# Routed attention and a feed-forward layer on one core: four late placements moved, and one batch's feed-forward pieces dealt unevenly

## The chip, the cores and the metric

The kernel runs on one NeuronCore of a Trainium2 chip. The core has a matrix engine (TensorE, PE in the profile), a vector engine (VectorE, DVE), a scalar engine (ScalarE, ACT), GpSimd (POOL) and a sync engine (SyncE, SP), which here only issues transfers. Each works through its own queue of instructions in the order in which they were written down, and engines wait for each other by semaphores. The metric is the device time of one execution in microseconds (us), and lower is better. The kernel before takes 940.79 us (median of 3 runs, 940.7 to 941.31).

## The reference

Two stages follow each other. The first is attention with routing: 4 batches, 8 heads, 768 tokens, 64 numbers per token and head. Every query and every key is assigned to the one of 16 centroids with which its direction agrees best, and a query attends only to keys of its own cluster.

```python
q_assign = np.argmax(np.einsum('bhsd,hcd->bhsc', q_n, c_n), axis=-1)
k_assign = np.argmax(np.einsum('bhsd,hcd->bhsc', k_n, c_n), axis=-1)
mask = q_assign[:, :, :, None] == k_assign[:, :, None, :]
scores = np.where(mask, scale * np.matmul(q, k.transpose(0, 1, 3, 2)), -1e9)
attn = softmax(scores)
x = np.matmul(attn, v)             # heads side by side: 3072 tokens x 512
h = x @ w_in                       # 512 -> 2048
g = np.maximum(h, 0.0) + alpha * np.minimum(h, 0.0)
out = g @ w_out                    # 2048 -> 512
```

The second stage is the feed-forward layer in the last three lines, with one slope alpha per hidden feature.

## The kernel before, in words

**Units of work.** Two heads at a time make a pair; there are 16 pairs, number n = 0 to 15, four to a batch. The pairs n = 9 to 15 are *sorted*: their tokens are first ordered by cluster (on DVE and PE), written to a scratch tensor in that order by indirect transfers of POOL, and read back by SP (`order_load`), so that a query needs only a window of keys. Before a sorted pair is scored, DVE turns its rows round (`order_blocks`, line 713), and after it its result goes back to the tokens' own order through another scratch tensor (`to_rows` on PE and ACT, `put_back` on POOL, `fetch_back` on SP, `turn_back` on DVE, line 1030).

**Steps, stretches and slots.** Attention is cut into steps u = 0 to 74. Three steps in a row treat one sorted pair, or one half of the queries of another pair; here these three steps are called a stretch. Batch 2's attention is steps 48 to 62, five stretches: pairs 9, 10 and 11, then the two halves of pair 8. Batch 3's is steps 63 to 74, pairs 12 to 15. A stretch begins with scores on PE (line 784), exponentials on ACT, the sums, inverses and products of the stretch before it, and masks on DVE (line 825). Then come 12 slots: two in its first step, five in each of the others. In a slot the loop at the kernel's end takes one item of `todo` (a mask, sums of exponentials, their transposition), then scatters of `sorting`, then some feed-forward pieces (`feed`), and things prepared for later pairs (`prepare`). `later` puts a piece some slots ahead.

**Feed-forward pieces.** They fill PE while the attention's other engines work. `ffn_pieces` gives 28 for half a batch: 16 pieces `hidden`, in two groups of 8 (four products of 128x128 by 128x384, line 1066, an ACT copy, line 1072, and a slope on DVE, line 1058, which is issued with the next hidden piece, and at once at every fourth one), and after each group 6 pieces `final` (four products by 128x512, line 1084; a token block takes two of them, and then the sum is taken out of PSUM). Below, h0 to h15 are the hidden pieces of batch 1's second half, and F0.0, F0.4 and so on its final ones: token block, first feature. These 28 pieces lie over batch 2's five stretches. The loop deals them evenly: `at_slot` and `places` say how far the stretches have come, and `pieces` how many are due; `kept` leaves two over. If a stretch ends between the two pieces of a token block, the second follows at once.

**The end.** The last batch's feed-forward is written with seven half-size products in place of eight (`last_pieces`): the `hidden(x)` products p1 to p7 for 8 pairs of feature blocks, of which p4 goes through the list `late` into the next block, then a piece `room_for_y`, then `final(t)` for three token blocks. `g_sums` and `w_out_sums` make, on DVE, the sums that these products need.

**What sets the order.** The schedule is manual: the order of the statements is the order of each engine's queue. `load_at` holds what is issued at a step's start (`load`, `load_v`, `order_load`), `prep_at` what is prepared at a slot. `ORDERS` names the step at which a sorted pair's rows are loaded for the ordering; the features follow one step later and the centroid products (`order_sims`, line 575) two. `order_load` is issued 3 or 4 steps ahead of the pair's first step. POOL's indirect transfers are paced: ACT writes a tiny tile (`pace`, line 651, 8 buffers), and POOL waits for it (line 652). Small PSUM tiles all come from one bank (`misc`), the feed-forward's from two (`ps_f`).

Of the kernel before, what the change touches and what calls it, by code (L numbers as in the profile page):

```python
# [16 lines left out]
ALU = mybir.AluOpType  # L17
# [6 lines left out]
def kernel(  # L24
# [80 lines left out]
    NO = WHOLE * NCH - 3  # L105
    NP = len(pairs)
# [619 lines left out]
    SB = NJ // GROUP  # L726
    assert NJ == GROUP * SB and SB == GT
    steps, begun_at, feeds = [], [], {}
    for b in range(B):
        whole = [n for n in range(b * NCH, (b + 1) * NCH) if n >= NO]  # L730
# [155 lines left out]
    parts, totals = {}, {}  # L886
# [255 lines left out]
    def last_pieces():  # L1142
# [72 lines left out]
            f = x + NQ * (i // 2)  # L1215
            return w_in_sb[:, KH * (i % 2):KH * (i % 2 + 1), f * P:(f + 1) * P]

        def g_sums(x):
            (t0, t1), (z0, z1) = g[x][0], g[NQ + x][0]
            S1, S2, S4 = (g_sum(x, m) for m in ("S1", "S2", "S4"))  # L1220
            for to, p, q, op in ((S1, t1, z1, ALU.add), (S2, S1, t0, ALU.subtract),
                                 (t1, t0, t1, ALU.subtract), (S4, z0, S2, ALU.subtract)):
                nc.vector.tensor_tensor(out=to, in0=p, in1=q, op=op)

        def w_out_sums(x):

            T1, T2, T3, T4 = (w_out_form(m, x) for m in ("T1", "T2", "T3", "T4"))
            B11, B12, B21, B22 = (
                w_out_sb[:, f, c0:c0 + HC].rearrange("p (a w) -> p a w", a=KH)
                for f in (x, NQ + x) for c0 in (0, HC))  # L1230
            for to, p, q in ((T1, B12, B11), (T2, B22, T1), (T3, B22, B12), (T4, B21, T2)):
                nc.vector.tensor_tensor(out=to, in0=p, in1=q, op=ALU.subtract)

        late = deque()
# [101 lines left out]
            return [p1, p5, p6, p2, p7, p3, p4]  # L1336

        def room_for_y():
            late.popleft()()
            t = sorts["xmore"].tile([P, NCH, HS], FP32, name="xT").rearrange(  # L1340
                "p c q -> p (c q)")
            ys.extend(ypool.tile([P, DM], FP32, name="y") for _ in range(HJ))
            ys.extend(t[:, i * DM:(i + 1) * DM] for i in range(HJ))
            for x in (NQ - 2, NQ - 1):
                g_sums(x)
            for x in (NQ - 2, NQ - 1):
                w_out_sums(x)
        pieces = []
        for x in range(NQ):
            pieces += hidden(x)  # L1350
# [15 lines left out]
    FREE = SLOTS * SB - 3  # L1366


    ORDERS = [26, 29, 35, 38, 41, 56, 59]
    prep_at, load_at = {}, {}  # L1370
    for (n, half), u in start_of.items():
        def at(step, slot, piece):
            prep_at.setdefault((step, slot), []).append(piece)
        if half is None:
            t = ORDERS[n - NO]
            load_at.setdefault(t, []).append(lambda n=n: load(n))
            for i in range(2):
                at(t + 1, FIRST + i, lambda n=n, i=i: order_features(n, i))
            at(t + 2, 2, lambda n=n: order_sims(n))
            load_at.setdefault(u - (3 if n in (NO + 1, NO + 2, NP - 1) else 4), []).append(  # L1380
                lambda n=n: order_load(n))
            at(u - 4, 0, lambda n=n: prep_clusters(n))
            for i in range(2):
                at(u - 1, i, lambda n=n, i=i: order_blocks(n, i))
                at(u - 1, FIRST + i, lambda n=n, i=i: order_queries(n, i))
            continue
        if half == 0:
            if n < NCH:
                if n > 1:
                    load_at.setdefault(max(u - 7, 0), []).append(lambda n=n: load(n))  # L1390
                if n > 0:
                    load_at.setdefault(max(u - 6, 0), []).append(lambda n=n: load_v(n))
            else:
                load_at.setdefault(u - 9, []).append(lambda n=n: load(n))
                load_at.setdefault(u - 7, []).append(lambda n=n: load_v(n))
            if n < NCH:
                for g in range(len(groups)):
                    at(u - 4, FIRST + g, lambda n=n, g=g: prep_features(n, g))
            else:
                for w in range(2):  # L1400
                    at(u - 7, FIRST + w + (u - 7 == TOGETHER - 1),
                       lambda n=n, w=w: prep_blocks(n, w))
            at(u - (3 if n < NCH else 5 if u - 6 < TOGETHER else 6), FIRST,
               lambda n=n: prep_sims(n)) if u - 6 < 2 * TOGETHER else at(
                   u - 6, FIRST + 1, lambda n=n: prep_sims(n))
            if n >= NCH:
                at(u - 4, FIRST if u - 4 < TOGETHER else 0, lambda n=n: prep_clusters(n))
        if n < NCH:

            if half == 1 or n == 0:  # L1410
                at(u - (3 if half else 1), FIRST,
                   lambda n=n, half=half: prep_queries(n, half, 0))
            continue
        for h in range(2):
            at(u - 1, FIRST + h, lambda n=n, half=half, h=h: prep_queries(n, half, h))
# [33 lines left out]
    def kept(u):  # L1449


        return {NS: 12, begun_at[-2]: 2, begun_at[-3]: 2}.get(block_end(u), 0)

    def block_end(u):
        return min(x for x in begun_at if x > u)

    def block_start(u):
        return max(x for x in begun_at if x <= u)
# [52 lines left out]
    for i in range(2 * NCH):  # L1511
        load_at.setdefault(TOGETHER + 2 + 2 * i, []).append(
            lambda i=i: keep_w_in(i // 2, i % 2 * DF // 2))
    todo = deque()
    for u in range(TOGETHER, NS + 1):
        for piece in load_at.get(u, []):
            piece()
        if u < NS:
            n, half, s = steps[u]
        if s == 0 or u == NS:  # L1520
            prior = steps[u - 1][:2]
            assert not unfinished[0]
            tick()
            if u < NS:
                score(n, half, range(0, NJ // 2), alone=NJ // 2 - 1)
            total(prior[0])
            tick()
            if prior[1] is None:
                invert(prior[0], 0, 1)
                weigh_near()  # L1530
            else:
                invert(*prior)
                weigh(GROUP if u == TOGETHER else NJ)
            if u < NS:
                for chunk in last(NJ // 2):
                    mask(chunk)
            if prior[1] is None:
                normalise_near(prior[0])
            else:
                normalise(*prior)  # L1540
            if u in begun_at:
                feed_block(u)
                if u < NS:
                    whole = len(ffn) - kept(u)
            if u == NS:
                break
            tick()
            score(n, half, range(NJ // 2, NJ), alone=NJ // 2)
            E = last(NJ)
            for c in range(NJ // 2, NJ):  # L1550
                todo.append(lambda c=c, E=E: mask(E[c]))
            if half is None:
                of = {c: e for _, _, c, e in E}
                todo += [lambda n=n, E=of: add_near(n, 0, E),
                         lambda n=n: (turn(n, 0), rows_sums(n, 0)),
                         lambda n=n, E=of: add_near(n, 1, E),
                         lambda n=n: (turn(n, 1), rows_sums(n, 1))]
                todo += [lambda: None] * 5
            else:
                todo.append(lambda E=E: add_up(E[1], E[0]))  # L1560
                for c in range(2, NJ):
                    todo.append(lambda c=c, E=E: add_up(E[c]))
                todo.append(lambda n=n, half=half: (turn(n, half), rows_sums(n, half)))
                todo += [lambda: None] * 3
            slots = range(3, SLOTS)
        else:
            slots = range(SLOTS)
        if u == TOGETHER + 1:
            order_constants()
        for i in slots:  # L1570
            tick()
            if s == 0:
                prepare(u, FIRST + i - 3)
            at_slot = (u - block_start(u)) // SB * FREE + (s * SLOTS + i - 3)
            places = (block_end(u) - block_start(u)) // SB * FREE
            pieces = len(ffn) - kept(u) + -whole * (places - 1 - at_slot) // places
            todo.popleft()()
            room = scatters_at(u - start_of[NO, None], s, i)
            if room and sorting:
                pace()  # L1580
            while sorting and room:
                scatters, piece = sorting.popleft()
                piece()
                room -= scatters
            feed(max(pieces, 0))
            if (s, i) == (SB - 1, SLOTS - 1) and unfinished[0]:
                feed(1)
            if s > 0:
                prepare(u, i)
# [227 lines left out]
```

## Time and profile before

| what | value |
|---|---|
| median of 3 runs | 940.79 us |
| the profiled execution | 941.51 us |
| its span, first to last instruction | 939.6 us |
| PE busy | 919.1 us (98%) |
| DVE busy | 656.2 us (70%) |
| POOL busy | 382.3 us (41%) |
| ACT busy | 262.8 us (28%) |
| granted TensorE clock, mean | 0.997 |

Times in the profile are us from the span's start. A row of the order of time names start, length, engine, line and operation, then the tile written and the tiles read, the shape, and how many instructions are merged; a bracket at the end says how long the engine stood idle before it and what it waited for. One product of 32-bit numbers appears as two instructions, so a hidden piece is x8 and takes about 2.65 us, and a final piece is x8 and takes about 3.45 us. PE's chain of waits and its busy time say the same here: where PE stands still, time is lost, and where another engine does, mostly none is.

Where the stretches lie in the profiled execution (from one score to the next): steps 48 to 50 at 438.5, 51 to 53 at 461.4, 54 to 56 at 494.6, 57 to 59 at 517.4, 60 to 62 at 544.2, and batch 3 from 575.9 on.

### The profile page before, as it was taken

The numbers are of one execution on the slowest core, as the hardware profiler recorded it, in microseconds if no ns is written. First come the engines' busy times: TensorE is split into PE (matmuls) and PEld (weight loads), VectorE is DVE, ScalarE is ACT, GpSimd is POOL, SyncE is SP. The second block draws the span as 40 slices with busy tenths as digits, with TensorE's granted clock in tenths as the row PEclk, the third lists the DMA queues.
The fourth block names the chain that finished last, engine by engine and source line by source line (L and its number), as shares of the span: only waits on it lengthen the run. The fifth ranks groups of instructions, "written<-read, shape, count | busy, mean of one in ns | idle before, by whom it ended". The sixth has DMA issues, their size and how long they took to land.

```text
span 939.6 us, 11988 instructions
## 1 busy us (share of the span) xinstructions
PE 919.1 (98%) x3963; PEld 495.3 (53%) x3963; DVE 656.2 (70%) x1246; ACT 262.8 (28%) x661; POOL 382.3 (41%) x580
## 2 busy tenths in 40 slices
PE   8999999999999999999999999999999999999997
PEld 5534444445455454454544544555555555556886
DVE  5797798799679589598987889754647135598100
ACT  5764444323023132231212332122212120221000
POOL 2333222200026677478575786668533471000000
PEclk9999999999999999999999999999999999999999
DMA  8433758039002635252952383662501012000000
GB/s 298 135 117 98 144 131 150 18 62 196 1 9 72 156 82 137 62 120 76 176 100 41 59 138 73 149 124 60 92 31 27 12 37 53 1 0 1 23 23 25
DMA packets 226708, 77.71 MB, mean 83 GB/s; under 512 B 210752, under 2 KB 214544, under 8 KB 226640
## 3 DMA queue, kind: packets, MB, share of 16 engines
q1 hardware_dynamic: 217728, 62.72, 30.9%
q0 software_dynamic: 8064, 13.78, 4.7%
q8 instruction: 33, 0.54, 0.2%
q10 hardware_dynamic: 848, 0.39, 0.2%
q14 instruction: 35, 0.29, 0.1%
HBM read 52.25 MB, written 24.25 MB: 81 GB/s over the span
## 4 chain that ended last, share of the span: by engine, by line
PE 82%; DVE 10%; SPq 3%; DMA 1%; issue 1%; POOL 1%; ACT 1%; DVEq 0%; POOLq 0%; ACTq 0%
PE fps L1084 24%; PE fps L1066 22%; PE sps L784 6%; PE vps L939 5%; PE sps L1244 4%; PE sps L1300 4%; PE vps L1244 2%; PE vps L1300 2%; PE fps L784 2%; SPq L697 1%; PE mps L972 1%; PE fps L1300 1%; PE fps L1244 1%; PE vps L972 1%; SPq L127 1%
## 5 line engine op out<-in xcount | busy, mean ns | idle before, releaser
L1066 PE MATMUL fps<-xT,w_in_sb 128*128 128x384 f32 x768 | 258.9, 490 | 0.0
L1084 PE MATMUL fps<-w_out_sb,gT 128*128 128x512 f32 x576 | 254.8, 596 | 2.5 <-DVE gT L1058 2.5
L675 POOL DMA_INDIRECT scratch<-stage,off x168 | 177.9, 1059 | 75.1 <-issue 29.6
L1066 PEld LDWEIGHTS fps<-xT,w_in_sb 128*128 128x128 f32 x768 | 142.5, 190 | 103.1 <-issue 4.3
L1084 PEld LDWEIGHTS fps<-w_out_sb,gT 128*128 128x128 f32 x576 | 107.4, 190 | 134.8 <-issue 121.4
L1072 ACT COPY gT<-fps 128x384 f32<-128x384 f32 x96 | 46.0, 479 | 236.2 <-PE fps L1066 236.2
L652 POOL COPY paced<-pace 1x1 f32<-1x1 f32 x205 | 51.2, 250 | 139.5 <-ACT pace L651 138.9
L1058 DVE SCALAR_TENSOR_TENSOR gT<-gT,alpha 128x384 f32<-128x384 f32 x96 | 61.2, 647 | 58.7 <-ACT gT L1072 58.5
L1011 POOL DMA_INDIRECT back<-rows,off x84 | 85.7, 1021 | 24.2 <-issue 18.6
L784 PE MATMUL sps<-qkT 64*128 64x384 f32 (+1 forms) x464 | 86.1, 490 | 0.4 <-DVE qkT L713 0.4
L805 ACT ACTIVATE E<-sps 128x768 f32<-128x768 f32 (+1 forms) x76 | 56.3, 786 | 62.6 <-PE sps L793 38.4
L784 PEld LDWEIGHTS sps<-qkT 64*128 64x128 f32 x464 | 41.8, 188 | 39.7 <-issue 14.6
L825 DVE SCALAR_TENSOR_TENSOR more<-aq,key,more 128x384 f32<-128x384 bf16 (+2 forms) x116 | 60.4, 577 | 0.0
L939 PE MATMUL vps<-E,vt 128*64 128x384 f32 x292 | 54.2, 495 | 1.5 <-DVE xT L1042 1.5
L271 POOL TENSOR_TENSOR w_in_sb<-w_in_sb,power 128x512 f32<-128x512 f32 x16 | 25.7, 1612 | 68.6 <-DVE w_in_sb L268 68.6
L825 DVE SCALAR_TENSOR_TENSOR E<-aq,key,E 128x384 f32<-128x384 bf16 (+2 forms) x88 | 45.3, 569 | 0.6 <-ACT E L802 0.6
L271 POOL TENSOR_TENSOR w_out_sb<-w_out_sb,power 128x512 f32<-128x512 f32 x16 | 22.5, 1412 | 56.0 <-DVE w_out_sb L268 56.0
L907 DVE RECIPROCAL inverses<-mps 64x12 f32<-64x12 f32 (+1 forms) x42 | 10.5, 249 | 48.1 <-PE mps L894 47.9
L835 DVE TENSOR_TENSOR acc<-acc,E 128x768 f32<-128x768 f32 x35 | 33.3, 951 | 14.6 <-ACT E L805 13.6
L1090 ACT COPY y<-fps 128x512 f32<-128x512 f32 x18 | 10.6, 587 | 102.3 <-PE fps L1084 102.3
L1092 DVE TENSOR_TENSOR y<-y,fps 128x512 f32<-128x512 f32 x24 | 16.3, 680 | 28.5 <-PE fps L1084 28.5
L805 ACT ACTIVATE more<-sps 128x768 f32<-128x768 f32 (+1 forms) x40 | 29.2, 764 | 12.5 <-PE sps L784 11.6
(284 smaller groups left out, 1178.4 us busy)
## 6 DMA issues: line engine op xcount, KB each, us to landing
raw<-in_moe_w_in_dram SPq DMA_DIRECT2D x16, 512.0 KB
raw<-in_moe_w_out_dram SPq DMA_DIRECT2D x16, 512.0 KB
out_dram<-y SPq DMA_DIRECT2D x21, 256.0 KB
qk<-scratch SPq DMA_DIRECT2D x56, 96.0 KB
qk<-in_q_dram SPq DMA_DIRECT2D x48, 96.0 KB
qk<-in_k_dram SPq DMA_DIRECT2D x48, 96.0 KB
w_in_kept<-w_in_sb SPq DMA_DIRECT2D x8, 512.0 KB
vt<-in_v_dram SPq DMA_DIRECT2D x9, 384.0 KB
```

Of the source, the lines that this page charges most:

```text
L652: nc.gpsimd.tensor_copy(out=sorts["paced"], in_=token)
L675: nc.gpsimd.indirect_dma_start(out=scratch[n][1][h * NX + xx], out_offset=bass.IndirectOffsetOnAxis(ap=ranks[n][:, xx, h:h + 1], axis=0), ...
L784: nc.tensor.matmul(out=bank(ps, h, m), lhsT=qkT[r:r + D, S + c * P:S + (c + 1) * P], rhs=qkT[r:r + D, tokens], start=True, stop=not early_ ...
L805: nc.scalar.activation(out=E[:, :, 0:m], in_=ps[:, :, 0:m], func=AF.Exp, scale=SCALE)
L825: nc.vector.scalar_tensor_tensor(out=e, in0=of, scalar=keys[n][:, NJ + c, h:h + 1], in1=e, op0=ALU.is_equal, op1=ALU.mult)
L939: nc.tensor.matmul(out=po[r:r + D, 0:HS], lhsT=vts[n][:, h, c, :], rhs=e[:, h, :], start=(c == 0), stop=(c == NJ - 1))
L1011: nc.gpsimd.indirect_dma_start(out=to[i], out_offset=bass.IndirectOffsetOnAxis(ap=place[:, h, j:j + 1], axis=0), in_=rows[j // HJ][:, j % ...
L1058: nc.vector.scalar_tensor_tensor(out=gs[f], in0=gs[f], scalar=alpha[:, f:f + 1], in1=gs[f], op0=ALU.mult, op1=ALU.max)
L1066: nc.tensor.matmul(out=ps[:, 0:HS], lhsT=w_in_sb[:, c, f * P:(f + 1) * P], rhs=xTs[b, half][:, c, :], start=(c == 0), stop=(c == NCH - 1))
L1084: nc.tensor.matmul(out=ps[:, 0:DM], lhsT=gs[f][:, i * P:(i + 1) * P], rhs=w_out_sb[:, f, :], start=on and f == f0, stop=off and f == f0 + ...
L1244: nc.tensor.matmul(out=bank[to], lhsT=w_in_form(m, x, cc), rhs=rhs[:, cc, :], start=start and cc == 0, stop=cc == KH - 1, skip_group_check ...
L1300: nc.tensor.matmul(out=bank[to], lhsT=g_form(m, x, t), rhs=w_out_form(n, x), start=start and x == 0, stop=x == NQ - 1, skip_group_check=no ...
```

## The change

Five things change.

1. `ORDERS`: pair 15 is loaded for its ordering at step 60, where it was step 59. Its features and centroid products move along, to steps 61 and 62, and what follows them too.
2. `LEADS` replaces a condition on n. It gives the same leads, except that `order_load` of pair 11 is issued 4 steps ahead (start of step 50) where it was 3 (start of step 51).
3. `room_for_y` no longer issues the last hidden block's product p4. The first result product, p1 of `final(0)`, comes ahead of it and then empties `late`.
4. The sums for the last two feature blocks, 16 DVE instructions that `room_for_y` issued block by block, go into `late` as 8 pairs, in the order in which the products need them; p1 of `final(0)` issues them behind p4.
5. `shares` deals the 28 pieces of batch 1's second half with weights 10:7:8:12:13 over the five stretches of batch 2, in place of evenly.

```diff
-        def g_sums(x):
+        def g_sums(x, parts=range(4)):
...
-            for to, p, q, op in ((S1, t1, z1, ALU.add), (S2, S1, t0, ALU.subtract),
-                                 (t1, t0, t1, ALU.subtract), (S4, z0, S2, ALU.subtract)):
+            sums = ((S1, t1, z1, ALU.add), (S2, S1, t0, ALU.subtract),
+                    (t1, t0, t1, ALU.subtract), (S4, z0, S2, ALU.subtract))
+            for to, p, q, op in [sums[i] for i in parts]:
...
         def room_for_y():
-            late.popleft()()
...
-            for x in (NQ - 2, NQ - 1):
-                g_sums(x)
-            for x in (NQ - 2, NQ - 1):
-                w_out_sums(x)
+            late.extend(lambda i=i, x=x: (g_sums(x, [i]), w_out_sums(x, [i]))
+                        for i in range(4) for x in (NQ - 2, NQ - 1))
...
-    ORDERS = [26, 29, 35, 38, 41, 56, 59]
+    ORDERS = [26, 29, 35, 38, 41, 56, 60]
+    LEADS = [4, 3, 4, 4, 4, 4, 3]
...
-            load_at.setdefault(u - (3 if n in (NO + 1, NO + 2, NP - 1) else 4), []).append(
+            load_at.setdefault(u - LEADS[n - NO], []).append(
                 lambda n=n: order_load(n))
...
+    shares = {start_of[NO, None]: (10, 7, 8, 12, 13)}
...
-            at_slot = (u - block_start(u)) // SB * FREE + (s * SLOTS + i - 3)
-            places = (block_end(u) - block_start(u)) // SB * FREE
-            pieces = len(ffn) - kept(u) + -whole * (places - 1 - at_slot) // places
+            weights = shares.get(block_start(u), (1,) * ((block_end(u) - block_start(u)) // SB))
+            at = (u - block_start(u)) // SB
+            left = (sum(weights[at + 1:]) * FREE
+                    + weights[at] * (FREE - 1 - (s * SLOTS + i - 3)))
+            pieces = len(ffn) - kept(u) + -whole * left // (sum(weights) * FREE)
```

`w_out_sums` gets the same argument `parts` as `g_sums`.

More of the change, by code (lines that the diff above doesn't have):

```diff
@@ L1216, in w_out_form, with w_out_sums @@
             return w_in_sb[:, KH * (i % 2):KH * (i % 2 + 1), f * P:(f + 1) * P]
-        def g_sums(x):
+        def g_sums(x, parts=range(4)):
             (t0, t1), (z0, z1) = g[x][0], g[NQ + x][0]
             S1, S2, S4 = (g_sum(x, m) for m in ("S1", "S2", "S4"))
-            for to, p, q, op in ((S1, t1, z1, ALU.add), (S2, S1, t0, ALU.subtract),
-                                 (t1, t0, t1, ALU.subtract), (S4, z0, S2, ALU.subtract)):
+            sums = ((S1, t1, z1, ALU.add), (S2, S1, t0, ALU.subtract),
+                    (t1, t0, t1, ALU.subtract), (S4, z0, S2, ALU.subtract))
+            for to, p, q, op in [sums[i] for i in parts]:
                 nc.vector.tensor_tensor(out=to, in0=p, in1=q, op=op)
-        def w_out_sums(x):
+        def w_out_sums(x, parts=range(4)):
             T1, T2, T3, T4 = (w_out_form(m, x) for m in ("T1", "T2", "T3", "T4"))
@@ L1230, in w_out_sums @@
                 for f in (x, NQ + x) for c0 in (0, HC))
-            for to, p, q in ((T1, B12, B11), (T2, B22, T1), (T3, B22, B12), (T4, B21, T2)):
+            sums = ((T1, B12, B11), (T2, B22, T1), (T3, B22, B12), (T4, B21, T2))
+            for to, p, q in [sums[i] for i in parts]:
                 nc.vector.tensor_tensor(out=to, in0=p, in1=q, op=ALU.subtract)
```

## The prediction

> **What bounds the kernel.** I read the page first, then PE's waits, then busy times by stretch, then the order of time around each wait.
>
> ```profile
> PE 919.1 (98%) x3963; PEld 495.3 (53%) x3963; DVE 656.2 (70%) x1246; ACT 262.8 (28%) x661; POOL 382.3 (41%) x580
> ```
>
> PE is the bound: of 939.6 us it stands still for 20.5. PE's waits from 457 to 600 us list 7.8 of them. The busy times of the stretches of steps 51-53, 54-56, 57-59 and 60-62 (PE, PEld, DVE, ACT, POOL, clock):
>
> ```profile
> 461.40:494.63 33.23, 30.05 (x133) 15.80 (x132) 27.85 (x52) 8.28 (x24) 20.14 (x32) 0.98 0.61 113
> 494.63:517.42 22.79, 22.79 (x97) 11.62 (x97) 16.37 (x35) 6.49 (x22) 13.88 (x22) 0.95 0.26 47
> 517.42:544.17 26.75, 25.69 (x125) 14.35 (x125) 22.39 (x41) 10.56 (x39) 20.90 (x32) 1.00 0.41 68
> 544.17:575.90 31.73, 29.73 (x115) 13.93 (x114) 28.94 (x53) 8.00 (x30) 23.95 (x38) 1.00 0.67 114
> ```
>
> In the second and fifth stretch DVE is nearly as full as PE. PE's waits in the order of time:
>
> ```profile
> 492.11 2.59 PE L1084 MATMUL fps<-w_out_sb,gT 128*128 128x512 f32 x4 [2.29 <-DVE gT L1058]
> 560.35 1.07 PE L575 MATMUL mps<-qk,cT 128*32 128x384 f32 x8 [1.34 <-issue]
> 578.47 0.80 PE L784 MATMUL fps<-qkT 64*128 64x320 f32 x2 [0.71 <-ACT E L802]
> 586.22 0.58 PE L601 MATMUL mps<-simT,row 128*128 128x1 f32 x4 [0.83 <-DVE simT L589]
> 859.91 1.56 PE L1244 MATMUL sps<-vt,w_in_sb 128*128 128x384 f32 x4 [0.65 <-DVE gT L1179]
> ```
>
> The first, at 489.8, is a late transfer seen through DVE's queue: F0.4 wants the slope of h7, which stands behind two transpositions of pair 11, and these behind its loads, which SP issued only at 482.4:
>
> ```profile
> 487.35 0.98 DVE L713 STREAM_TRANSPOSE qkT<-qk 128x768 f32<-128x768 f32 x1 [1.44 <-DMA qk<-scratch]
> 490.13 0.98 DVE L713 STREAM_TRANSPOSE qkT<-qk 128x768 f32<-128x768 f32 x1 [1.80 <-DMA qk<-scratch]
> 491.45 1.14 DVE L1058 SCALAR_TENSOR_TENSOR gT<-gT,alpha 128x384 f32<-128x384 f32 x2
> ...
> 482.36 4.61 SPq L697 DMA_DIRECT2D qk<-scratch x8
> ```
>
> From 493.4 to 496.6 the granted clock is 0.50: F0.4's x4 took 2.59 where half of a usual x8 (3.45) takes 1.72, and the scores after it lost 1.04.
>
> **The Trainium skill.** "TensorE: Matmul & The Clock Gate", Part 1, says that a window of about 3.4 us in which PE was idle halves its clock for the next. The trace agrees: half a clock for some 3.4 us after the 2.29 us gap, and none after gaps of 1.5 us or less. The same page ("Architectural detail") calls ACT's and DVE's queues strictly first in, first out; the late slope above shows that here.
>
> **The deal.** Pieces due after a slot are 28 times the weight passed, rounded down. Even: 5, 7, 4, 6, 6 by stretch (the 7th by the rule on an unfinished block). New: 5, 4, 5, 6, 8. The first stretch keeps its slots. The second keeps h3 to h6 and loses h7, F0.0, F0.4: PE work of 2.65+3.45+3.45 = 9.55 us, of which the third gets h7 (+2.65, finals stay four), the fourth two finals for two hidden (+1.60), the fifth two hidden more (+5.30). The sum is 0: only waits can change.
>
> **Second stretch.** `order_load` of pair 11 leaves SP's queue about 15 us sooner: past two sets of stage loads (L661) and `load_v`, right after the store at 465.7. Its buffers are free (pair 10's transpositions ended at 459.9), so it lands near 476 (last issue of eight near 472, plus the 3.6 of the chain's row) and DVE no longer waits 3.24. SP's stage loads come up to 1 us later, some scatters up to 2: POOL's late scatters wait for nobody before 479, and nothing on PE waits for them.
> But PE has too little left. At 469.75 the scores are over. The next on PE is L383, whose bank is read by DVE until 470.86; h3, which stood ahead of it, now stands behind (first slot to second). L383 0.75 and h3 2.65 end at 474.35; ACT's copy and hand-over 0.62. DVE: from 470.85 masks 0.92+1.06, a slope 0.53, and then it waits for h3's copy until 474.97. From there slope 0.53, the five of the argmax 2.65, mask 0.72, sums and transpositions 1.53+1.88+1.46+1.87, a slope 0.53, both L713 1.86: 488.0. The next stretch's scores start there, at 488.1, not 494.63: 6.5 us sooner with 9.55 us less done, +3.05. In other words, of 18.35 us PE works 12.1 (L383 0.78, four hidden 10.6, transposes and clusters 0.75) and idles 6.2: some 1.2 ahead of L383, 1.8 ahead of L1002 (its bank is read by the argmax until 476.1), 0.8 ahead of the second L1002, 2.4 ahead of the scores. In its place go the 2.29 and the 0.87 that F0.4 lost to the clock.
>
> **Third and fourth.** No clock loss in the scores: -1.04. Third: PE 7.1+13.8+2.65+0.66 = 24.2 against DVE 17.6: PE-bound; `turn_back`'s transfer, for which DVE waited 2.94, comes sooner than DVE does. Fourth: L575 waited 1.06 for ACT (copy of h10, then rows); now it waits for the copy of F2.4's y, then rows, about 1.0: -0.05.
>
> **Fifth, and pair 15 a step later.** L601 of pair 14 waited 0.30 with nothing ahead of it; now h12 is ahead: -0.30. DVE stood 2.23+0.33 for pair 15's rows, then L575 1.34: the rows now have a whole step more, and stand in SP's queue behind one more set of stage loads (about 2 us): -1.34. PE has 5.3 us more to do here, DVE 0.6 more slope and about 1.9 of argmax less, so DVE is done with L713 near 569 when PE wants it at 575.9: -0.40 and -0.71 (the bank that F1's addition on DVE held). L601 of pair 15 lands between filler: -0.83. Cover: PE work of 35.0 against DVE's 29. If it were gone, these 3.6 us stay. The buffer that `fetch_back` of pair 11 takes is freed by L575 or L713, now near 568; its rows reach DVE by about 574, when DVE has 2 to 3 us to spare. Pair 15's scatters end at most a step (some 13 us) later; SP's load, at 657 before, would land near 681, and DVE asks for it at 693: nothing.
>
> **The end.** p4 waited 0.63 for the addition on its bank and ran 1.56 for 1.29; p1 of 3.45 us now covers that. p5 ran 0.15 long for the last w_out sum, which now comes after 4 sums, not 13: -1.05 in all. p1 needs the slopes of its own block only for its last two products. No instruction is added.
>
> **Sum.** +3.05-1.04-0.05-0.30-1.34-0.40-0.71-0.83-1.05 = -2.7 us. The profiled execution (941.51, of which 1.9 lie outside the span) would go to 938.8 (941.51-2.7); its distance to the median is kept, so 940.79-2.7 = 938.1, 0.28% faster. About 0.2% (1.9 us) is what a measurement here tells from no change.
> Bounds of what the trace doesn't show: the second stretch's idle time is 4.5 at best (h3's copy does not hold DVE up, 1.6 less) and 7.9 at worst (clock halved again, 1.7 more).
>
> **Rivals.**
> *Half clock stays.* The 2.4 us gap ahead of the scores at 488 is as long as the one that halved the clock. If it falls whole into one window, 1.7 us come back; if the 0.71 stays too (which bank is given is settled when the kernel is built), 938.1+2.4 = 940.5, no difference. For it: gap lengths. Against it: by the phase of before, only 1.6 of it lie in one window, and a window with 1.48 idle was left alone.
> *The pace holds ACT (slower).* In the fifth stretch ACT stood 2.59 and 2.45 us behind the 8 pace tiles, harmless ahead of finals; now h13 to h15 need ACT's copies there for their two banks. POOL has 20 scatters and 6 put-backs, 26 at 1.3 = 34 us, in a stretch of 35. If both holds reach PE, 938.1+5.0 = 943.1. It decides from 4.6 us of held PE on. Against it: POOL's queue of the fourth stretch starts 5 us sooner, with ACT.
> *The load isn't sooner.* If SP were held anyway, the 3.24 stay on DVE and 3.2 come back: 941.3, no difference. SP's free time from 466.7 to 472.9 speaks against it.
>
> **Numbers.** My forecast 0.54, half clock and load together 0.28, pace and other starvation 0.18. Low end 935.5: 1.6 less idle and 1 us more from DVE's slack; high end 943.0, at the pace rival, so that less than 2 in 10 is left out. The forecast's own range is 935.5 to 938.9. Faster 0.54, same 0.28, slower 0.18.
>
> **What would show it.** Right: pair 11's L697 issued at 466-473; no DVE wait for it; PE idle about 6 us between 469 and 488, in four gaps; scores of pair 11 near 488; no PE wait at L575 of pair 15, and hardly any from 540 to 600; p4 without wait after p1. Wrong: pace waits of ACT with PE waiting for ACT near 550-565, a clock of 0.5 after 488, a gap over 8 us in the second stretch, or PE waits after 600, where I expect none.

## The result and the profile after

The changed kernel takes 939.74 us (median of 22 runs, 938.0 to 940.99). The kernel before, run beside it, takes 941.11 us (22 runs, 939.2 to 942.77). The ratio is 0.9986, with a 95% interval of 0.998 to 0.9993: faster, by 1.4 us or 0.14%, which is half of what was forecast and less than the 0.2% that the prediction calls no change. The median lies in the range that was stated, 935.5 to 943.0, but above the 938.9 at which the forecast's own range ends. The profiled execution took 938.98 us, with a span of 937.2 us: 2.4 us less than the 939.6 of before.

The page of the changed kernel, busy times:

```profile
PE 916.9 (98%) x3963; PEld 495.1 (53%) x3963; DVE 656.3 (70%) x1246; ACT 262.7 (28%) x662; POOL 386.3 (41%) x581
```

The busy times by stretch, from one stretch's first scores to the next one's (PE, PEld, DVE, ACT, POOL, granted clock, DMA share, GB/s):

```profile
461.61:488.63 27.02, 20.01 (x109) 11.38 (x108) 24.02 (x46) 7.88 (x24) 17.28 (x26) 1.00 0.72 135
488.63:512.96 24.33, 24.33 (x104) 12.48 (x104) 20.46 (x42) 6.84 (x23) 18.99 (x31) 1.00 0.44 66
512.96:541.15 28.19, 27.39 (x125) 14.45 (x124) 23.12 (x42) 9.15 (x33) 21.08 (x32) 1.00 0.36 64
541.15:575.60 34.45, 34.45 (x131) 16.78 (x130) 29.98 (x52) 9.32 (x35) 24.03 (x36) 1.00 0.49 97
```

PE's standing still has moved into the second stretch: 27.02 less 20.01, 7 us. In the third to fifth, where it was 3.1 us before, it is now 0.8. Over the whole span PE stands still as long as before (20.3 us against 20.5). Its busy time is what became shorter, by 2.2 us, and most of that is the half clock after h7's slope, which cost 0.87 and 1.04 us before and is absent here. PE's waits in the order of time:

```profile
466.61 1.79 PE L972 MATMUL mps<-E,vt 128*64 128x384 f32 x16 [1.09 <-DVE inverses L907]
471.32 0.85 PE L383 MATMUL mps<-qkT,cT 128*32 128x384 f32 x8 [1.17 <-DVE qk L978]
476.67 0.55 PE L1002 MATMUL mps<-ident,qk 128*128 128x128 f32 x3 [1.72 <-DVE simT L404]
483.16 0.55 PE L1002 MATMUL mps<-ident,qk 128*128 128x128 f32 x3 [0.69 <-ACT every L448]
488.63 1.29 PE L784 MATMUL sps<-qkT 64*128 64x224 f32 x8 [2.34 <-DVE qkT L713]
529.13 1.06 PE L575 MATMUL mps<-qk,cT 128*32 128x384 f32 x8 [0.80 <-ACT rows L1005]
578.17 0.80 PE L784 MATMUL fps<-qkT 64*128 64x320 f32 x2 [0.71 <-ACT E L802]
```

From 471 to 489 these are four gaps of 5.92 us in all. The wait of 2.29 us for h7's slope, the half clock after it, the waits of pair 15's L575 and L601 and that of p4 are gone. Only the 0.71 in the last row stayed. DVE's and SP's rows say why DVE is no longer late for pair 11, and what it then waits for:

```profile
475.50 0.62 DVE L1058 SCALAR_TENSOR_TENSOR gT<-gT,alpha 128x384 f32<-128x384 f32 x1 [1.65 <-ACT gT L1072]
...
486.74 1.83 DVE L713 STREAM_TRANSPOSE qkT<-qk 128x768 f32<-128x768 f32 x2
...
467.82 6.46 SPq L697 DMA_DIRECT2D qk<-scratch  x8
```

The load is issued 14.5 us sooner and L713 waits for nothing. At the end, p4 follows p1 with no bracket:

```profile
861.39 1.45 PE L1246 MATMUL sps<-vt,w_in_sb 128*128 128x384 f32 x4
```

**Where the 2.4 us came from.** Measured from the start of the second stretch, so that small differences before it drop out, the scores of pair 11 come at 27.02 us (33.23 before), those of pair 12 at 114.03 (114.54), those of pair 13 at 158.62 (159.99), and the products p5 and p6 of the first result piece (the two groups of 16 in a row, L1302) are over at 411.43 (413.87). So three places gain: 0.5 us up to pair 12, 0.9 in the stretch after it, 1.05 at the end. All that moved in the five stretches, with its 9.55 us of PE work carried from one to others, is worth 0.5 us.

### The profile page after: what moved, and what is told of

It is laid out like the page before. It is cut to its first block, busy times and chain, and to the rows that moved or that the text cites. A ratio compares the mean times of both kernels' runs of the same rounds, so it can differ in the third digit from the quotient of the medians.

```text
span 937.2 us, 11992 instructions
## 1 busy us (share of the span) xinstructions
PE 916.9 (98%) x3963; PEld 495.1 (53%) x3963; DVE 656.3 (70%) x1246; ACT 262.7 (28%) x662; POOL 386.3 (41%) x581
## 4 chain that ended last, share of the span: by engine, by line
PE 88%; DVE 6%; SPq 2%; issue 1%; ACT 1%; DMA 1%; POOL 0%; ACTq 0%; DVEq 0%; POOLq 0%
PE fps L1084 26%; PE fps L1066 24%; PE sps L784 7%; PE vps L939 6%; PE sps L1302 4%; PE sps L1246 4%; PE fps L784 2%; PE vps L1246 2%; PE vps L1302 2%; PE fps L1302 1%; PE fps L1246 1%; PE vps L972 1%; PE mps L972 1%; PE sps L793 1%; PE mps L383 1%
## 5 line engine op out<-in xcount | busy, mean ns | idle before, releaser
L675 POOL DMA_INDIRECT scratch<-stage,off x168 | 180.8, 1076 | 89.5 <-issue 30.0
L1072 ACT COPY gT<-fps 128x384 f32<-128x384 f32 x96 | 45.9, 478 | 239.7 <-PE fps L1066 239.7
L784 PE MATMUL sps<-qkT 64*128 64x384 f32 (+1 forms) x464 | 85.0, 485 | 2.3 <-DVE qkT L713 2.3
L784 PEld LDWEIGHTS sps<-qkT 64*128 64x128 f32 x464 | 41.2, 186 | 40.8 <-issue 13.2
L1092 DVE TENSOR_TENSOR y<-y,fps 128x512 f32<-128x512 f32 x24 | 16.4, 682 | 28.7 <-PE fps L1084 28.7
```

Of the source, the lines that this page charges most:

```text
L675: nc.gpsimd.indirect_dma_start(out=scratch[n][1][h * NX + xx], out_offset=bass.IndirectOffsetOnAxis(ap=ranks[n][:, xx, h:h + 1], axis=0), ...
L784: nc.tensor.matmul(out=bank(ps, h, m), lhsT=qkT[r:r + D, S + c * P:S + (c + 1) * P], rhs=qkT[r:r + D, tokens], start=True, stop=not early_ ...
```

## The experiments

They ran on three chips, four kernels on each, beside the kernel before. On A and B that kernel itself takes 949.1 and 949.4 us, on C 941.1, as in the first measurement. The chip of that one, called the first chip here, isn't on record, and it could be C. A ratio is only compared with others of the same chip.

| kernel | chip | median us (runs) | ratio to before, 95% interval |
|---|---|---|---|
| all placements, pieces dealt evenly | A | 959.17 (6) | 1.0106 [1.0065, 1.0147] |
| pair 11's load alone | A | 946.75 (14) | 0.9979 [0.9955, 1.0002] |
| pair 15's ordering alone | A | 960.02 (6) | 1.0117 [1.0086, 1.0148] |
| the end alone | A | 948.41 (14) | 0.9989 [0.9967, 1.0011] |
| the change | B | 953.08 (22) | 1.0048 [1.0033, 1.0063] |
| all placements, dealt evenly | B | 955.24 (9) | 1.0083 [1.005, 1.0115] |
| the change, h3 a slot sooner | B | 955.04 (9) | 1.0065 [1.0042, 1.0088] |
| before, with fill | B | 953.33 (13) | 1.0036 [1.0014, 1.0059] |
| the change | C | 940.12 (22) | 0.9988 [0.9982, 0.9994] |
| the change without the move of pair 15's ordering | C | 938.48 (11) | 0.9974 [0.9964, 0.9983] |
| the uneven deal alone | C | 945.18 (6) | 1.0045 [1.0032, 1.0059] |
| pair 11's load and the end | C | 936.5 (6) | 0.9952 [0.9939, 0.9965] |

### First chip (A): the parts one by one

All placements, with the deal made even again:

```diff
-    shares = {start_of[NO, None]: (10, 7, 8, 12, 13)}
+    shares = {start_of[NO, None]: (1, 1, 1, 1, 1)}
```

> The change with the deal left even (weights 1:1:1:1:1). If the deal costs time because it starves PE while DVE is full in the second stretch, this is faster than the change: no wait for pair 11's loads (2.29 us) and no half clock after it (1.9), no wait at L575 of pair 15 (1.34) and at its L601 (0.83), the end 1.05 shorter; together 6.5 to 8 us less than before, near 933.5 us, a ratio near 0.992. If the deal is what makes the change faster, this run is no faster than the change, near 940 us.

Pair 11's load alone:

```diff
-            load_at.setdefault(u - (3 if n in (NO + 1, NO + 2, NP - 1) else 4), []).append(
+            load_at.setdefault(u - (3 if n in (NO + 1, NP - 1) else 4), []).append(
```

> Only pair 11's load one step earlier. If that load stands ahead of a slope in DVE's queue: the scores of pair 11 come near 491.4 in place of 494.6, at full clock, 3.2 to 4.3 us less than before, a ratio near 0.996. If SP was held anyway, or DVE is full without it: within 0.1% of before.

Pair 15's ordering alone:

```diff
-    ORDERS = [26, 29, 35, 38, 41, 56, 59]
+    ORDERS = [26, 29, 35, 38, 41, 56, 60]
```

> Only pair 15's ordering one step later. If DVE stood for its rows and PE behind it: L575 of pair 15 without its wait of 1.34, no wait of 0.83 at its L601, nor the 0.40 at L713: 2.0 to 2.6 us less than before, a ratio near 0.9975. If the load is only as late again (it stands one set of stage loads further back on SP): within 0.1%.

The end alone: the changed kernel with `ORDERS` ending in 59, pair 11's lead 3 and even shares.

> Only the end: first result product ahead of p4, sums in the order of need. p4 without its wait of 0.65, the first five result products ending 1.05 us sooner, everything before the end the same: 1.05 us less, a ratio near 0.9989. If the end is set by the stores or by DVE, nothing.

**Measured.** The load alone gave 0.9979 and the end alone 0.9989, both with 1 just inside the interval; the wait of 2.29 us for h7's slope is gone in the first of them, which was expected near 0.996. Both kernels with pair 15's ordering moved and an even deal came out about 1% slower, where 0.992 and 0.9975 were expected. In the one that moves nothing else, PE's two waits after the scores of pair 12, and DVE's rows ahead of them:

```profile
578.87 0.80 PE L784 MATMUL fps<-qkT 64*128 64x320 f32 x2 [1.28 <-ACT E L802]
582.09 0.62 PE L894 MATMUL mps<-part,fold 128*128 128x24 f32 x2 [2.41 <-DVE simT L404]
```

```profile
580.53 1.04 DVE L1030 STREAM_TRANSPOSE xT<-qk 128x384 f32<-128x384 f32 x2 [5.54 <-DMA qk<-back]
581.49 0.54 DVE L404 STREAM_TRANSPOSE simT<-mps 128x384 f32<-128x384 f32 x1
```

This is a chain through two shared things, a bank and a queue. L575 of pair 15, a step later, fills the one `misc` bank at 571.4. DVE empties it with L404, but L404 stands in DVE's queue behind L1030, and L1030 waits 5.54 us for a transfer. So L894, which wants the same bank, waits until 582.1. In the changed kernel L1030 waited 1.65 us and L404 ran at 574.29, ahead of the stretch's end. The difference begins on POOL. SP holds the transfer until pair 11's last `put_back` has landed, and POOL, which works there with hardly a pause, starts that one 2.3 us ahead of the scores of pair 12 here (573.44), 8.4 ahead of them in the kernel before and 12.0 in the changed one (563.63). On B it is 2.3 with all placements and an even deal, and 12.1 in the change, so the deal is what gives POOL its lead. The third to fifth stretch together last 87.0 us in the changed kernel, and 78.5 with the even deal. Pair 15's L575 and L601 no longer wait in this experiment either (1.34 and 0.83 us before). The deal alone removes those waits too (chip C, below), so each of the two edits does it by itself, and the move without the deal brings larger ones.

**What stays aside.** All of chip A's traces have waits that no trace of the first chip has: here and there, a good half of it between 630 and 680 us, ACT or DVE stands still for something that the profile calls remote, and PE with it (PE 9.06 us at one place in the first of these four; DVE 13.10 and PE 5.23 in the last). So the 1% is not the size of the chain above, and the end's 0.9989 carries such a stand as well. This led to the second set, with the change itself in it.

### Second chip (B): the change again, and two waits in the second stretch

The changed kernel as it is, and all placements with an even deal as above:

> The changed kernel once more, beside the three below on one chip. The profile of the change: scores of pair 11 near 488.6, four gaps of 6 us together in the second stretch, no wait of PE from 590 to the end's p4; a ratio near 0.9986. If the two runs that moved pair 15's ordering under an even deal (1.011) show a cost of that move, and the uneven deal only hides it, this run keeps 0.9986; if the cost belongs to the chip they ran on, this one shows it as well when it falls on such a chip.

> The change with an even deal, once more. In the first run of it ACT stood 6 to 10 us at line 1072 near 655 to 676 us, for nothing that the profile names, and PE 9.1 us behind it. If that stands with the chip, it is gone here where the kernel before runs near 941 us, and the run is 6 to 8 us faster than before, near 0.993. If it stands with pair 15's later ordering under an even deal, the ratio is again near 1.01.

Weights that bring h3 one slot sooner, ahead of L383, so that DVE needn't wait for its copy behind L383:

```diff
-    shares = {start_of[NO, None]: (10, 7, 8, 12, 13)}
+    shares = {start_of[NO, None]: (107, 63, 80, 120, 130)}
```

> The change with weights 107:63:80:120:130: the same pieces in each stretch, but h3 one slot earlier, ahead of L383, and h4 ahead of the first L1002. If the second stretch is bound by DVE's queue, which stands 1.65 us for h3's copy, the scores of pair 11 come 1.6 us sooner, near 487.0, and the gaps ahead of L383 and L1002 (1.17 and 1.72) are gone from PE: 1.6 us less than the change. If pair 11's scores wait for something else, they stay near 488.6 and the time is that of the change.

The kernel before, with three products that nobody reads ahead of the last part of F0.4, to keep PE's clock up (in the loop of `final`):

```diff
+                if (b, half, i, f) == (1, 1, 0, NF // 2 - 1):
+                    fill = ps_v.tile([P, 512], FP32, name="vps")
+                    for _ in range(3):
+                        nc.tensor.matmul(out=fill[:, 0:HS], lhsT=ident,
+                                         rhs=w_in_sb[:, 0, 0:HS], start=True, stop=True)
```

> The kernel before with three products of nobody's use (128x128 by 128x384, some 1.9 us on PE) put ahead of F0.4's fourth, where PE stands 2.29 us. If that gap halves PE's clock in most executions and costs them 1.7 to 1.9 us, the clock stays at 1.00 to the end and the time falls by about 1.2 us (ratio 0.9987), and its executions lie closer together. If the half clock costs nothing or comes rarely, the time is that of before (or 0.2 us more for the fill).

**The change is slower here**, by 0.48%, where it was faster by 0.14% on the first chip. Its stretches look as on the first: scores of pair 13 are at 159.97 us from the second stretch's start, against 158.62. What differs comes after. ACT's row, and PE's right behind it:

```profile
662.19 0.48 ACT L1072 COPY gT<-fps 128x384 f32<-128x384 f32 x1 [10.24 <-remote]
```

```profile
662.72 4.25 PE L1066 MATMUL fps<-xT,w_in_sb 128*128 128x384 f32 x8 [6.70 <-issue]
```

ACT stood 10.24 us ahead of this copy; PE, whose two banks these copies empty, stood 6.70 us, and two windows there ran at half clock. Waits of ACT marked remote are in each of the eight traces of A and B, and in none of the six from the first chip and C. And they go with one edit: in the five kernels of A and B that move pair 15's ordering, the longest at these copies (L1072, between 657 and 676 us) is 9.05, 9.99, 10.24, 10.67 and 9.27 us; in the three that don't, it is 3.66, none and 3.71. All five are slower than before by 0.48% or more, the three by 0.36% at most. On A the move alone is enough for the loss (1.0117). On B the slower kernels share it but differ from the kernel before in more, and the fill, without the move, is slower too (1.0036). Why the move lengthens the stand, and what ACT stands for, isn't settled by these runs; that the stand is the whole of the 8 us by which these chips are slower isn't shown either; and the change without the move wasn't tried on them.

**h3 a slot sooner.** The gaps ahead of L383 and of the first L1002 vanish, and the scores wait longer in their place:

```profile
488.56 2.40 PE L784 MATMUL sps<-qkT 64*128 64x224 f32 x8 [4.31 <-DVE qkT L713]
```

They come 26.29 us after the start, where the change has 27.02 on the first chip and 27.10 on C: 0.7 to 0.8 us sooner, half of the 1.6 that was expected. (On this chip the change has 28.10, but ACT stood 6.32 and 1.75 us on remote in that stretch.) DVE still waits for h3's copy, only less than the 1.65 us of the change:

```profile
474.32 0.62 DVE L1058 SCALAR_TENSOR_TENSOR gT<-gT,alpha 128x384 f32<-128x384 f32 x1 [0.69 <-ACT gT L1072]
```

And the idle time now lies in one piece, two windows run at half clock (2.40 for 1.29), and by the scores of pair 12 the gain is gone (115.66, against 114.03 on the first chip and 115.70 on C).

**Fill.** It missed its place:

```profile
493.30 1.13 PE L1089 MATMUL fps<-w_out_sb,gT 128*128 128x512 f32 x2 [2.17 <-DVE gT L1058]
494.26 3.79 PE L1087 MATMUL vps<-w_in_sb,ident 128*128 128x384 f32 x6
```

PE waits for the slope one product sooner than assumed, so the fill (L1087) ran behind the wait and at half clock, 3.79 us long. The scores of pair 11 come at 35.45 us (33.23 before, on the first chip). So this run says nothing about the price of the half clock, and what a fill inside the gap would do to the clock stays untried.

### Third chip (C): which parts carry the gain

> The changed kernel once more, beside the three that follow. If the move of pair 15's ordering is what lets ScalarE stand at its copies of the result pieces near 650 to 676 us (theory A), this one shows such a stand of 5 us or more and a ratio of 1.003 to 1.006 where the kernel before shows some too, and a ratio of 0.997 to 0.999 on a chip where neither has it. If any change of the instruction stream moves the stand about (theory B), the stand is there or not without regard to the chip's time for the kernel before.

The change without the move of pair 15's ordering:

```diff
-    ORDERS = [26, 29, 35, 38, 41, 56, 60]
+    ORDERS = [26, 29, 35, 38, 41, 56, 59]
```

> The change without its move of pair 15's ordering (last ordering one step earlier again, all else as changed). By the prediction's sum pair 15's ordering meets the fifth stretch again: the wait of PE for VectorE's similarities there returns (0.5 to 2 us), L601 of pair 15 waits some 1 us, and the time is 1 to 3 us above the changed kernel's. Theory A: ScalarE's stand near 650 to 676 us is gone or under 3 us, and the time is 3 to 7 us below the changed kernel's on a chip that shows the stand. Theory B: the stand is there within 2 us of the changed kernel's.

The uneven deal alone: `ORDERS` ending in 59, pair 11's lead 3, the end as before.

> The shares 10:7:8:12:13 alone: loads, last ordering and the end as before. By the prediction's sum the second stretch then has no room for pair 11: its load is late and its pieces are fewer, so the scores of pair 11 wait 4 us or more longer than before; the fifth stretch, with pair 15's ordering and most pieces, shows waits of PE of 1 to 3 us. Time 3 to 7 us above the kernel before. A rival holds that the shares carry the gain themselves: 1 to 2 us below the kernel before.

Pair 11's load and the end together: the edit of the one before last, and even shares.

```diff
-    shares = {start_of[NO, None]: (10, 7, 8, 12, 13)}
+    shares = {start_of[NO, None]: (1, 1, 1, 1, 1)}
```

> Pair 11's load earlier and the end's sums spread, with even shares and pair 15's ordering where it was: the two parts that alone gave ratios of 0.998 and 0.999. If they add up, 0.9965 to 0.998, and below the changed kernel on the same chip by 3 to 7 us where that one shows ScalarE's stand, by 0 to 1.5 us where it doesn't. If they don't add up (the stand moves to wherever the stream is changed, theory B), 0.9985 to 1.003.

**Measured.** ACT never stands on remote on this chip, and the order is plain: load and end alone 936.5 us, with the deal 938.48, with the deal and the move 940.12, before 941.1, the deal alone 945.18. The two small parts are worth 4.6 us; the deal takes 2.0 of them back, and the move of pair 15's ordering 1.6 more. Two expectations were missed: without the move the kernel was to be 1 to 3 us slower than the change, and the load and the end were to give 0.9965 at best. In the deal alone the time came as expected, but PE's waits of 1 to 3 us in the fifth stretch did not: PE never waits there. In times from the second stretch's start (rows of the scores, L784):

| kernel | scores of pair 11 | of pair 12 | of pair 13 |
|---|---|---|---|
| before (first chip) | 33.23 | 114.54 | 159.99 |
| the change (first chip) | 27.02 | 114.03 | 158.62 |
| the change | 27.10 | 115.70 | 160.29 |
| without the move | 27.17 | 114.18 | 157.26 |
| the deal alone | 30.49 | 120.26 | 163.53 |
| load and end | 30.34 | 110.88 | 156.32 |
| all placements, even deal (B) | 30.41 | 108.93 | 159.29 |

*Why the load suffices.* Load and end, stretches two and five:

```profile
462.10:492.40 30.30, 29.13 (x133) 15.83 (x132) 27.62 (x52) 8.29 (x24) 19.44 (x31) 1.00 0.63 122
...
540.91:572.90 31.99, 29.72 (x115) 13.92 (x114) 28.94 (x53) 7.94 (x30) 24.23 (x38) 1.00 0.62 113
```

```profile
486.75 1.83 DVE L713 STREAM_TRANSPOSE qkT<-qk 128x768 f32<-128x768 f32 x2
```

With the load sooner, DVE is done with pair 11 at 488.58, and PE, still with its seven pieces, asks at 492.40: 3.8 us of slack, no wait, no half clock. The deal takes 9.55 us of PE's work out of this stretch. Only the first 3.8 of them do any good; the other 5.7 turn into idle time, about the 5.92 us of gaps above.

*What the deal alone lacks.* Without the sooner load:

```profile
483.62 4.71 SPq L697 DMA_DIRECT2D qk<-scratch  x8
```

```profile
488.72 0.98 DVE L713 STREAM_TRANSPOSE qkT<-qk 128x768 f32<-128x768 f32 x1 [1.69 <-DMA qk<-scratch]
491.56 0.98 DVE L713 STREAM_TRANSPOSE qkT<-qk 128x768 f32<-128x768 f32 x1 [1.85 <-DMA qk<-scratch]
```

```profile
492.59 2.40 PE L784 MATMUL sps<-qkT 64*128 64x224 f32 x8 [6.14 <-DVE qkT L713]
```

The scores wait 6.14 us and two windows run at half clock. Here too DVE is late because its load is, and with fewer pieces PE has less to do until then.

*What the move costs once the deal is there.* Nothing waits for pair 15's ordering in the version without the move: no bracket at its L575 or L601, nor at the scores of pair 12. So there the deal has already done what the move was to do, as it has in the deal alone. The 1.5 us between the two versions lie in one spot right after the scores of pair 12. The change on the first chip, then the version without the move:

```profile
576.77 0.70 PE L784 MATMUL fps<-qkT 64*128 64x320 f32 x2
578.17 0.80 PE L784 MATMUL fps<-qkT 64*128 64x320 f32 x2 [0.71 <-ACT E L802]
578.90 0.40 PE L894 MATMUL mps<-part,fold 128*128 128x24 f32 x2
```

```profile
577.30 0.70 PE L784 MATMUL fps<-qkT 64*128 64x320 f32 x4
577.93 0.40 PE L894 MATMUL mps<-part,fold 128*128 128x24 f32 x2
```

All four of these products take 0.70 us together when none waits. When two must wait for ACT to have read the first two's result, each pair takes 0.70 to 0.80 by itself: the bracket says 0.71, and the loss up to L894 is 1.5. That the wait comes from which of the two feed-forward banks is handed out there fits the rows, and wasn't tried apart.

*Why the median gained less than the trace.* The change's profile on C has the same four gaps as on the first chip, but a span 1.8 us longer. Three clock windows around the scores of pair 11, on C and then on the first chip (columns as above):

```profile
485.72:489.13 3.41, 1.02 (x8) 0.51 (x8) 3.38 (x7) 1.02 (x4) 3.09 (x5) 1.00 0.07 19
489.13:492.54 3.41, 3.41 (x14) 1.78 (x12) 2.41 (x4) 2.23 (x6) 2.94 (x7) 0.50 0.08 22
492.54:495.95 3.41, 3.41 (x34) 2.03 (x32) 3.36 (x9) 0.04 (x1) 2.14 (x5) 1.00 0.09 26
```

```profile
483.69:487.10 3.41, 2.60 (x9) 1.19 (x7) 3.34 (x7) 0.78 (x3) 3.09 (x5) 1.00 0.21 60
487.10:490.51 3.41, 1.88 (x13) 1.19 (x14) 3.38 (x7) 1.33 (x4) 3.08 (x6) 1.00 0.07 19
490.51:493.92 3.41, 3.41 (x34) 2.15 (x34) 3.36 (x8) 1.07 (x5) 2.96 (x5) 1.00 0.10 29
```

On C the gap of 2.39 us falls whole into one window, and the next runs at 0.50: 1.7 us. On the first chip a gap of 2.34 us straddles an edge, 0.8 and 1.53, and nothing happens. "TensorE: Matmul & The Clock Gate", Part 1, of the Trainium skill calls the window free-running, with 3413 ns, and these two traces agree: the same gap in the same kernel costs 1.7 us or none, by its place against the window.

## Why the prediction was right or wrong

**The direction and the steps.** Nearly every step stood. Pair 11's load was issued at 467.8 (466 to 473 predicted), DVE no longer waited for it, PE stood still 5.92 us in four gaps (6.2 in four: 1.2, 1.8, 0.8, 2.4, measured 1.17, 1.72, 0.69, 2.34), and the scores came at 488.63 (488.1, in a trace that starts the stretch 0.2 later). L575 of pair 14 waited 0.80 for ACT (1.0 predicted). The waits of 0.30, 1.34, 0.40, 0.83 went, and the end gained its 1.05. The sum for the trace, -2.7, came out at -2.4. What came out at half is the median.

**The term that failed.** "-0.71", the bank that F1's addition held, stayed at 0.71. DVE's addition (L1092) is over at 576.72 in the changed kernel, where it was at 580.48, so it no longer holds a bank when the two products start at 578.17. They wait for ACT all the same. In the version without the move the addition is over at much the same time (576.97), and they do not wait. So freeing the bank sooner was not enough, which the rival with "settled when the kernel is built" had allowed for. And the term was mis-sized: by the version that lacks it, it costs 1.5 us, because it also parts products that otherwise run together. The step took a bracket for the whole price.

**The terms that were in part luck.** "Half clock stays" was given as a case of its own, with 1.7 us for a gap that falls whole into one window. It is in fact a mixture: both outcomes occur, execution by execution. The forecast's place, by the phase of before, was right for one profile and wrong for the next. The same holds for the saving. The sum takes the half clock of before (0.87 and 1.04) in full, because the one profile of it shows it. Each run's mean clock tells how often it occurs. The end of the span costs 0.2 to 1.5 us of clock in the six traces of the first chip and C, so a mean of 0.997 or less (2.3 us lost) needs a half-clock window besides, and one of 0.999 or more leaves no room for its 1.7. On C the kernel before then has the window in 17 of 32 executions, not in 12 (their mean time is 940.3 us, against 941.6), and 3 stay open. The change has it in 7 of 22, not in 8, and 7 stay open. So of the 1.9 us only 1.0 to 1.2 are saved on average, and 0.5 to 1.1 come back. That is an estimate from these counts. Put on the -2.4 between the two profiles, it leaves 0.4 to 1.1 us, where the medians on C differ by 1.0 (1.4 on the first chip).

**The cause given for pair 15.** "The rows now have a whole step more: -1.34" named only one of two edits that do it. Without the move, under the same deal, L575 of pair 15 waits for nothing either. "Cover: PE work of 35.0 against DVE's 29" is the part that holds by itself; the move adds nothing to it here and costs 1.6 us. The warning beside it, that `fetch_back` of pair 11 gives DVE 2 to 3 us to spare, held, narrowly: the rows came at 573.3 (about 574 predicted), DVE waited 1.65 us for them and PE not at all. Under an even deal DVE waited 5.5, and PE behind it.

**The rival on the other side.** "The pace holds ACT" did not come: PE never waits for ACT between 541 and 575 us in the changed kernel. On chip B the change is slower all the same, as its relatives are on A, and there PE waits behind ACT, but 100 us later, and in kernels that move pair 15's ordering; the profile names remote, not pace. No step of the prediction covered that.

**What was not asked.** The prediction added up one total. Its own figures held the better kernel. The sooner load removes the 2.29 and both losses to the clock (4.2 us in all), the end its 1.05. The deal and the move bring 6.2 us of gaps against 3.6 of savings, a loss of 2.6. The +3.05 of the sum hid this, because the load's 2.29 and 0.87 were already taken off in it. Added by edit rather than by place, the figures would have said that the load and the end alone are worth more than the whole, 5.25 against 2.7. Measured on C, it is 4.6 against 1.0.

## What to carry to other kernels

Add up a change's terms by edit as well as by place: two edits that carry each other's costs can hide that the rest alone is better. Filler work taken out of a stretch only helps up to the slack of the next engine (here 3.8 us of 9.55); past that it comes back as gaps, and a gap of two thirds of a clock window is priced once for itself and once, in some of the executions, for the half clock after it. And a bracket on a split group of small products can stand for twice its length. A loss that one profile shows can be absent from other executions of the same kernel, and then its removal saves only a part of it on average.

## What the runs showed of the hardware

- The same kernel before took 941.1 us in the first measurement and on C, and 949 on A and B, and the sign of this change went with it: 0.9986 and 0.9988 on the faster ones, 1.0048 on B. The traces of the slower ones show ACT standing up to 10.7 us on something called remote, longest where pair 15's ordering is moved; those of the faster ones never. Why is open.
- A window of 3.41 us in which PE stood still 1.95 us or more was followed by one at half clock in every trace here (from 300 to 930 us of the span). Windows with 1.5 to 1.93 us idle, in a stretch of full clock, were followed by one in two cases (1.55 in the end alone, 1.76 in the change on B) and by none in the others, more than ten. So a window that is idle as a whole, as the prediction puts it, isn't needed.
- Four products of 64 rows took 0.70 us together, and two of them 0.70 to 0.80 alone.
